# Attention scores in split precision: a low-by-low product left out, the low part taken in half-height products, and one division moved from DVE to GpSimd

## The chip, the cores and the metric

The kernel runs on one core of a Trainium2 chip. The metric is the device time of one execution in microseconds (us), lower is better. Engines are named as in the profile: PE is TensorE (its weight loads are listed apart as PEld), DVE is VectorE, ACT is ScalarE, POOL is GpSimd, SP issues most of the DMA transfers.

## The reference

Attention with a learned bias on the relative position, followed by two feed-forward layers, in float32:

```python
batch, n_heads, seq, head_dim = (2, 8, 576, 64)

scores = scale * np.matmul(q, k.transpose(0, 1, 3, 2))
x = (psi_rel / psi_i)[..., None]                     # positions only
bias = np.maximum(x @ w1 + b1, 0.0) @ w2
scores = scores + bias.transpose(2, 0, 1)[None]
scores = scores - np.max(scores, axis=-1, keepdims=True)
attn = np.exp(scores)
attn = attn / (np.sum(attn, axis=-1, keepdims=True) + 1e-09)
x = np.matmul(attn, v)                               # to (1152, 512)

g = x @ w_gate                                       # 512 -> 1536
x = (g / (1 + np.exp(-g)) * (x @ w_val)) @ w_out     # 1536 -> 512
h = x @ w_in                                         # 512 -> 2048
out = (np.maximum(h, 0) + np.log1p(np.exp(-np.abs(h)))) @ w_out2
```

## The kernel before

The program has three stages: the bias over positions (the first 55 us or so), attention, and the two feed-forward layers. The last two thirds are a long run of matmuls on PE (lines 722, 771 and 1080), whose order on PE is written out by hand; in attention the order on all engines is.

**Units and chunks.** A unit is one pair of heads of one batch element; there are eight. The queries of a unit go in two halves (`sub` 0 and 1), and a half is cut into chunks of 128 query rows against all 576 keys: four in the first half, five in the second, of which one (`"mix"`) takes the last 64 rows of both heads. So a unit has eight regular chunks and one mix chunk. A chunk's scores stand in a PSUM tile `ps` of two banks, one for each 288 keys (`hf` 0 and 1, `HALF` is 288).

**Precision.** A float32 matmul takes PE two instructions. The first two units (`i < PLAIN`) do that: `plain_scores` (line 313) multiplies the 64 head dimensions as they are. Inputs arrive with the 64 dimensions twice, in partitions 0 to 63 and again in 64 to 127, so one product runs in the upper half of the PE array (for `hf` 0) while one runs in the lower (for `hf` 1). From the third unit on, values are split into a high part and a remainder (the low part) in `float32r`, a form that PE multiplies in one instruction. `ql` and `qh` hold the low and high part of the queries, each twice over the 128 partitions. The key tile `kst` holds high parts in one half of the partitions and low parts in the other: for keys 0 to 287 the high parts lie in partitions 0 to 63, for keys 288 to 575 in partitions 64 to 127. A product of `ql` or `qh` over all 128 partitions thus adds the products with the keys' high and low parts in one go. `kst` and `ql` get their low parts from POOL (line 197).

**A slot.** `run_slot` issues one chunk: its scores on PE (`scores`, line 340), what DVE does with them (line 363: bias, scale and row maximum, PSUM to SBUF as `e`), the exponential of the chunk before on ACT (line 377), the sum and its reciprocal on DVE (381, 384), and the division of the row by its sum (line 388), which is on POOL but for one chunk. Then PE transposes pieces of a chunk that is three slots older (`pt`, line 414), ACT or DVE copy them to SBUF (`at`, line 421), and when all pieces of a half are there, PE multiplies them by the values (`po`, line 441). `finish` (lines 461 to 498) reads `po` out. The PSUM pool of `ps` has two tiles, that of `po` one. On PE, scores are thus always followed by transposes, except for the very last chunk, which is followed by `po`.

**Array shapes.** In the rows below, a matmul's first numbers are the partitions that it contracts over and the columns of the array that it uses. Scores of the plain units are 64x128 (two side by side), those of later units and transposes 128x128, `po` 128x64 (two side by side), the bias stage 128x32 (four side by side).

**The end of attention.** The last unit's half 1 has its fifth chunk (`n == 4`) divided on DVE. Behind that, in DVE's order, stand `t` and `B21l` (line 461), which read the `po` of half 0, a copy of transposed pieces (421), and the conversion of the first feed-forward weights (693, 696).

Of the kernel before, what the change touches and what calls it, by code (L numbers as in the profile page):

```python
# [15 lines left out]
ALU = mybir.AluOpType  # L16
# [3 lines left out]
P = 128  # L20
B, H, S, D, HID = 2, 8, 576, 64, 32
NP = H // 2
# [29 lines left out]
HALF = S // 2  # L52
# [47 lines left out]
def rows(w, f):  # L100

    return w.bitcast(I32)[P * f : P * (f + 1)].rearrange("p (k f) -> p k f", k=NK)
# [3 lines left out]
def tile_kernel(ctx: ExitStack, tc, qT, kT, vS, vT, wg, wv, wo, wi, wo2, table, out):  # L106
    nc = tc.nc
# [23 lines left out]
    with ExitStack() as actx:  # L131
# [166 lines left out]
        def plain_scores(u, n):  # L298


            sub, pr = u["sub"], u["pr"]
            ch = u["chunks"][n]
            ps = psS.tile([P, 2, 512], F32, tag="S", name="ps")
            if ch[0] == "mix":
                parts, bt = [(0, 0, 512), (1, 1, 256), (0, 1, 512), (1, 0, 256)], bias[4][:, pr]
            else:
                a, c = ch
                o, bt = 256 * sub + D * (sub and a) + P * c, bias[2 * sub + c][:, 2 * pr + a]
                parts = [(a, hf, o) for hf in range(2)]
            for a, hf, o in parts:  # L310
                rows = slice(D * hf, D * (hf + 1))
                to, m = (slice(D * a, D * (a + 1)), D) if ch[0] == "mix" else (slice(None), P)
                nc.tensor.matmul(  # L313
                    ps[to, hf, :HALF],
                    u["qr"][rows, a, o : o + m],
                    u["kr"][rows, a, HALF * hf : HALF * (hf + 1)],
                    start=True,
                    stop=True,
                )
            return ps, bt  # L320

        def scores(u, n):

            if u["i"] < PLAIN:
                return plain_scores(u, n)
            sub, pr, kst = u["sub"], u["pr"], u["kst"]
            ch = u["chunks"][n]
            ps = psS.tile([P, 2, 512], F32, tag="S", name="ps")
            if ch[0] == "mix":
                heads = [(0, 256), (1, 320)]  # L330
                bt = bias[4][:, pr]
            else:
                a, c = ch
                heads = [(a, (448 if sub else 256) * a + P * c)]
                bt = bias[2 * sub + c][:, 2 * pr + a]

            parts = [(t, a, o) for t in ("ql", "qh") for a, o in heads]
            for hf in range(2):
                for i, (t, a, o) in enumerate(parts):
                    nc.tensor.matmul(  # L340
                        ps[:, hf, :HALF],
                        u[t][:, o : o + P],
                        kst[:, a, HALF * hf : HALF * (hf + 1)],
                        start=i == 0,
                        stop=i == len(parts) - 1,
                    )
            return ps, bt

        marks = {}
# [25 lines left out]
        def softmax(u, n):  # L375
            e, sm = u["es"][n][:, :S], u["sm"]
            nc.scalar.activation(e, e, AF.Exp, bias=sm[:, 0, n : n + 1], scale=-1.0, accum_out=u["sums"][:, n, :1])  # L377
            for batch in BATCHES[u["sub"]]:
                if batch[-1] == n:
                    cols = slice(batch[0], n + 1)  # L380
                    nc.vector.tensor_reduce(
                        out=sm[:, 1, cols], in_=u["sums"][:, cols], axis=mybir.AxisListType.X, op=ALU.add
                    )
                    nc.vector.reciprocal(sm[:, 2, cols], sm[:, 1, cols])  # L384
                    for i in batch:
                        e = u["es"][i][:, :S]
                        eng = nc.vector if u["i"] == 2 * NP - 1 and n == 4 else nc.gpsimd
                        eng.tensor_scalar(e, e, sm[:, 2, i : i + 1], 1.0, op0=ALU.mult, op1=ALU.mult)  # L388

        made = [0, 0]  # L390

# [139 lines left out]
        def run_slot():  # L531
            nonlocal turned, done, prep, before, slot
            got = None
            if slot < len(chunks):
                i, sub, n = chunks[slot]
                if n == 0:
                    for _ in prep:
                        pass
                    if (i, sub) == (1, 0):
                        load_v(units[1])  # L540
                    elif (i, sub) == (0, 1):
                        units.append(load_k(2))
                    elif sub and i + 1 < 2 * NP:
                        load_q(units[i + 1])
                        if i > 1:
                            load_v(units[i + 1])
                        prep = itertools.chain(prepare_k(units[i + 1]), prepare_q(units[i + 1], 0))
                    elif i > 1 and not sub:
                        if i + 1 < 2 * NP:
                            units.append(load_k(i + 1))  # L550
                        if i == 2:
                            load_v(units[2])
                            units[2][0].update(v=units[2]["v"], vt=units[2]["vt"])
                        prep = prepare_q(units[i], 1)
                    if i < PLAIN:
                        job(units[i], sub)
                    if i == NP and sub == 0:
                        flat = lambda ap: ap.rearrange("p a s -> p (a s)")
                        pairs[2:] = [flat(bias[c][:, 2 * a : 2 * a + 2]) for a in range(2) for c in (2, 3)]
                        mixes[1] = flat(bias[4][:, :2])[:, : 5 * P]  # L560
                        nc.gpsimd.memset(mixes[1][:, S:], 0.0)
                u = units[i][sub]
                got = scores(u, n) if slot < len(chunks) - 1 else None
# [10 lines left out]
            if before:  # L574
                softmax(*before)
                before = None
# [14 lines left out]
            if slot == len(chunks) - 2:  # L591
                i, sub, m = chunks[-1]
                biased(units[i][sub], m, *scores(units[i][sub], m))
                softmax(u, n)
                softmax(units[i][sub], m)
# [497 lines left out]
    with tc.manual_schedule(engines={E.PE}):  # L1093
        quads = {"z": z}
        for q in range(4):
# [5 lines left out]
            for word in f"{OTHER if q else FIRST} {TAIL}".split():  # L1101
                who, what = word
                if who in "tu":
                    n = int(what)
                    if ws is None:
                        ws = convert(first + 2, outs[0]) + convert(first + 3, outs[1])
                    if q == 3 and n == 4:
                        t = TOKENS[n][0]
                        a = acc[t // 2][:, t % 2]
                        for at in (slice(0, DM // 2), slice(DM // 2, DM)):  # L1110
                            if who == "t":
                                held[n, at.start] = wide()[:, 0]
                            ps = held[n, at.start]
# [9 lines left out]
                    for i, t in enumerate(TOKENS[n]):  # L1123
                        if who == "t":
                            continue
                        a, ps = acc[t // 2][:, t % 2], held[n][:, i]
# [57 lines left out]
```

## Time and profile before

| | |
|---|---|
| three runs | 585.14, 585.31, 585.14 us; median 585.14 |
| the profiled execution | 585.39 us, of which 583.6 us from its first to its last instruction |
| attention with split products | 77.3 to 169.3 us of the span |
| end of attention | 169.3 to 184.5 us |
| feed-forward layers | 184.5 to 583.6 us |
| PE busy | 573.3 us (98% of the span), at the full granted clock |

Times in the rows count from the start of the span. PE's instructions overlap in the array, so a busy time is no sum of costs: what an instruction costs is the distance from its start to the start of the next one.

### The profile page before, as it was taken

What the parts mean: (1) busy time and instruction counts of PE and PEld (TensorE: products, weight loads), DVE (VectorE), ACT (ScalarE), POOL (GpSimd) and SP (SyncE); (2) the same over time, 40 slices, a digit from 0 to 9 for tenths busy, and PEclk for the clock granted to TensorE, in tenths of its full rate; (3) what the DMA queues carried; (4) which work ended last, traced back from release to release, by engine and by line L of the source; (5) the groups of instructions that cost most, each with busy time, mean ns of one, the idle gap of its engine ahead of it and who ended that gap; (6) DMA issues with size and microseconds to landing.
All of it is one profiled execution on the core that took longest, in us unless ns stands there. A gap on an engine that the chain in (4) does not pass through costs nothing.

```text
span 583.6 us, 11330 instructions
## 1 busy us (share of the span) xinstructions
PE 573.3 (98%) x4282; PEld 504.9 (87%) x4282; DVE 445.2 (76%) x958; ACT 377.1 (65%) x717; POOL 104.1 (18%) x160
## 2 busy tenths in 40 slices
PE   8999999999999999999999999999999999999997
PEld 5334588888888999999999999999989989988986
DVE  7999677778789989978879626589998876974432
ACT  7999888888887867656568325369727715733520
POOL 1002588898890000000000000000000000000000
PEclk9999999999999999999999999999999999999999
DMA  8999624233233342332343231222243241310013
GB/s 309 213 206 211 168 82 129 88 112 113 72 109 112 113 138 74 108 109 74 112 142 110 79 120 45 103 87 73 85 164 114 73 144 36 111 36 1 1 51 113
DMA packets 42039, 63.32 MB, mean 108 GB/s; under 512 B 4096, under 2 KB 30976, under 8 KB 41984
## 3 DMA queue, kind: packets, MB, share of 16 engines
q1 hardware_dynamic: 41984, 62.59, 36.9%
q8 instruction: 34, 0.56, 0.4%
q14 instruction: 21, 0.17, 0.1%
HBM read 49.60 MB, written 2.36 MB: 89 GB/s over the span
## 4 chain that ended last, share of the span: by engine, by line
PE 86%; ACT 6%; DVE 3%; DMA 2%; issue 1%; POOL 1%; DVEq 0%; ACTq 0%; POOLq 0%
PE pw L771 38%; PE pw L1080 17%; PE pw L722 13%; PE po L441 6%; PE ps L340 5%; PE pt L414 4%; ACT early L289 2%; ACT r L267 2%; PE pb L277 2%; PE ps L313 1%; DMA bias<-early 1%; DVE e L363 1%; DVE r L269 1%; ACT e L377 1%; POOL e L388 1%
## 5 line engine op out<-in xcount | busy, mean ns | idle before, releaser
L1080 PE MATMUL pw<-oh,g2h 128*128 128x512 f32 (+1 forms) x148 | 56.9, 384 | 0.0
L1080 PE MATMUL pw<-oh,g2l 128*128 128x512 f32 (+1 forms) x148 | 56.9, 384 | 0.0
L1080 PE MATMUL pw<-ol,g2h 128*128 128x512 f32 (+1 forms) x148 | 56.8, 384 | 0.0
L722 PE MATMUL pw<-gl,sh 128*128 128x384 f32 x144 | 48.2, 335 | 0.0
L722 PE MATMUL pw<-gh,sl 128*128 128x384 f32 x144 | 48.2, 334 | 0.0
L722 PE MATMUL pw<-gh,sh 128*128 128x384 f32 x144 | 48.2, 334 | 0.0
L696 DVE SCALAR_TENSOR_TENSOR x<-raw,x 128x512 int32<-128x512 int32 x68 | 46.2, 687 | 0.8
L277 PE MATMUL pb<-r,G 128*32 128x288 f32 x576 | 43.2, 416 | 3.4 <-ACT early L289 0.8
L363 DVE CUSTOM_DVE_ANT_0 e<-ps,bias 128x576 f32<-128x576 f32 x44 | 33.0, 751 | 16.3 <-PE ps L340 11.3
L388 POOL TENSOR_SCALAR e<-e,sm 128x576 f32<-128x576 f32 x43 | 33.1, 778 | 60.1 <-DVE sm L384 45.4
L269 DVE TENSOR_SCALAR r<-G 128x576 f32<-128x576 f32 x96 | 42.0, 522 | 0.0
L277 PEld LDWEIGHTS pb<-r,G 128*32 128x32 f32 x576 | 16.8, 110 | 28.9 <-ACT early L289 16.5
L421 ACT COPY at<-pt 128x512 f32<-128x512 f32 (+2 forms) x69 | 36.4, 550 | 7.5 <-PE pt L414 7.3
L441 PE MATMUL po<-at,v 128*64 128x256 f32 (+3 forms) x384 | 36.8, 332 | 1.3 <-issue 1.3
L340 PE MATMUL ps<-kst,ql 128*128 128x288 f32 x120 | 36.8, 335 | 0.5 <-POOL ql L197 0.4
L377 ACT ACTIVATE e<-e,sm 128x576 f32<-128x576 f32 x44 | 34.3, 780 | 2.9 <-DVE sm L363 1.4
L1130 DVE TENSOR_TENSOR acc<-pw,acc 128x512 f32<-128x512 f32 x26 | 16.8, 685 | 23.6 <-PE pw L1080 23.6
L693 DVE TENSOR_SCALAR x<-x 128x512 int32<-128x512 int32 x68 | 28.4, 423 | 8.4 <-ACT x L691 5.0
L441 PEld LDWEIGHTS po<-at,v 128*64 128x64 f32 x384 | 26.9, 137 | 8.2 <-issue 3.5
L1080 PEld LDWEIGHTS pw<-oh,g2l 128*128 128x128 f32 x148 | 27.8, 188 | 5.6
L1080 PEld LDWEIGHTS pw<-ol,g2h 128*128 128x128 f32 x148 | 27.8, 188 | 5.1
L1080 PEld LDWEIGHTS pw<-oh,g2h 128*128 128x128 f32 x148 | 27.8, 188 | 5.0
(274 smaller groups left out, 1677.3 us busy)
## 6 DMA issues: line engine op xcount, KB each, us to landing
raw<-in_wo_dram SPq DMA_DIRECT2D x28, 512.0 KB, 3.5
bias<-early SPq DMA_DIRECT2D x32, 288.0 KB, 8.4
raw<-in_wi_dram SPq DMA_DIRECT2D x16, 512.0 KB, 4.0
raw<-in_wv_dram SPq DMA_DIRECT2D x12, 512.0 KB, 4.2
raw<-in_wg_dram SPq DMA_DIRECT2D x12, 512.0 KB, 3.5
qr<-in_qT_dram SPq DMA_DIRECT2D x7, 576.0 KB, 3.8
bias<-in_kT_dram SPq DMA_DIRECT2D x6, 576.0 KB, 4.5
v<-in_vS_dram SPq DMA_DIRECT2D x8, 384.0 KB, 3.2
```

The costliest lines, as they stand in the source:

```text
L269: nc.vector.tensor_scalar(r, src[:, w0 : w0 + S], PB[:, n : n + 1], 0.0, op0=ALU.add, op1=ALU.max)
L277: nc.tensor.matmul(pb[32 * ct : 32 * ct + 32, hf, :HALF], W2, rs[ct][:, HALF * hf : HALF * (hf + 1)], start=True, stop=True,)
L340: nc.tensor.matmul(ps[:, hf, :HALF], u[t][:, o : o + P], kst[:, a, HALF * hf : HALF * (hf + 1)], start=i == 0, stop=i == len(parts) - 1,)
L363: nc.vector.tensor_tensor_reduce(out=e[:, :S].rearrange("p (a n) -> p a n", a=2), in0=ps[:, :, :HALF], in1=bt.rearrange("p (a n) -> p a n" ...
L377: nc.scalar.activation(e, e, AF.Exp, bias=sm[:, 0, n : n + 1], scale=-1.0, accum_out=u["sums"][:, n, :1])
L388: eng.tensor_scalar(e, e, sm[:, 2, i : i + 1], 1.0, op0=ALU.mult, op1=ALU.mult)
L421: marks[eng, u["i"], u["sub"]] = copy(at[:, :w], pt[:, :w]).ins
L441: nc.tensor.matmul(u["po"][D * a : D * (a + 1), o : o + n], v[:, D * t : D * (t + 1)], at[:, i : i + n], start=piece == 0 and o == 0, stop ...
L696: nc.vector.scalar_tensor_tensor(yi, lw, 29, yi, op0=ALU.logical_shift_right, op1=ALU.bitwise_or)
L722: nc.tensor.matmul(ps[:, :n], w[:, k], x, start=first and k == 0 and i == 0, stop=last and k == NK - 1 and i == 2)
L771: nc.tensor.matmul(ps[:, hf, :HALF], a[:, o + k], b[:, HALF * hf : HALF * (hf + 1)], start=start and k == 0 and i == 0, stop=k == 1 and i ...
L1080: nc.tensor.matmul(ps[:, at], g, w.rearrange("p k f -> p (k f)")[:, at], start=f == 0 and i == 0, stop=f == 3 and i == 2)
```

## The change

In `scores`, `qh` now comes ahead of `ql`, the loop over `hf` is the inner one, and `ql` is multiplied only in the 64 partitions in which `kst` holds high parts: the product of the low parts of queries and keys is left out. For `hf` 0 this is a product in the upper half of the array, for `hf` 1 in the lower, each into its own PSUM bank. The number of matmuls is the same. In `softmax`, the one division that was on DVE goes to POOL like the others.

```diff
@@ scores
-            parts = [(t, a, o) for t in ("ql", "qh") for a, o in heads]
-            for hf in range(2):
-                for i, (t, a, o) in enumerate(parts):
-                    nc.tensor.matmul(
-                        ps[:, hf, :HALF],
-                        u[t][:, o : o + P],
-                        kst[:, a, HALF * hf : HALF * (hf + 1)],
-                        start=i == 0,
-                        stop=i == len(parts) - 1,
-                    )
+            for t, rows in ("qh", lambda hf: slice(None)), ("ql", lambda hf: slice(D * hf, D * (hf + 1))):
+                for i, (a, o) in enumerate(heads):
+                    for hf in range(2):
+                        nc.tensor.matmul(
+                            ps[:, hf, :HALF],
+                            u[t][rows(hf), o : o + P],
+                            kst[rows(hf), a, HALF * hf : HALF * (hf + 1)],
+                            start=t == "qh" and i == 0,
+                            stop=t == "ql" and i == len(heads) - 1,
+                        )
@@ softmax
-                        eng = nc.vector if u["i"] == 2 * NP - 1 and n == 4 else nc.gpsimd
-                        eng.tensor_scalar(e, e, sm[:, 2, i : i + 1], 1.0, op0=ALU.mult, op1=ALU.mult)
+                        nc.gpsimd.tensor_scalar(e, e, sm[:, 2, i : i + 1], 1.0, op0=ALU.mult, op1=ALU.mult)
```

Lines behind the second edit move up by one: 414 becomes 413, 441 becomes 440, 461 becomes 460.

PE in the third unit, a regular chunk, transposes, the mix chunk (its two heads together) and the transposes behind it. Before:

```order
L340 MATMUL ps<-kst,ql 128x288
L340 MATMUL ps<-kst,qh 128x288
L340 MATMUL ps<-kst,ql 128x288
L340 MATMUL ps<-kst,qh 128x288
L414 MATMUL pt<-ident,e_898 128x128 x4
L340 MATMUL ps<-kst,ql 128x288 x2
L340 MATMUL ps<-kst,qh 128x288 x2
L340 MATMUL ps<-kst,ql 128x288 x2
L340 MATMUL ps<-kst,qh 128x288 x2
L414 MATMUL pt<-ident,e_897 128x128
```

The same place after the change:

```order
L340 MATMUL ps<-kst,qh 128x288 x2
L340 MATMUL ps<-kst,ql 128x288 x2
L413 MATMUL pt<-ident,e_898 128x128 x4
L340 MATMUL ps<-kst,qh 128x288 x4
L340 MATMUL ps<-kst,ql 128x288 x4
L413 MATMUL pt<-ident,e_897 128x128
```

The rows name the shape of the result, so that they don't show the height: the `qh` products stay 128x128, the `ql` products are now 64x128, and what follows, a transpose, is 128x128 again.

DVE at the end of attention, from the last reciprocals on. Before:

```order
L381 TENSOR_REDUCE sm_103<-sums_107 128x1
L384 RECIPROCAL sm_103<-sm_103 128x1
L388 TENSOR_SCALAR e_116<-e_116,sm_103 128x576
L461 TENSOR_TENSOR t<-po,t2f 128x320
L461 TENSOR_TENSOR B21l<-po,B21h 128x320
L421 COPY at<-pt 128x512
```

POOL's last instructions after the change:

```order
L581 TENSOR_TENSOR T2l<-t2f,T2h 128x320
L387 TENSOR_SCALAR e_115<-e_115,sm_103 128x576 x2
L581 TENSOR_TENSOR T3l<-t3f,T3h 128x320
L387 TENSOR_SCALAR bias_84<-bias_84,sm_103 128x576
L387 TENSOR_SCALAR e_116<-e_116,sm_103 128x576 x2
```

DVE loses its row of line 388, and everything behind it moves up; POOL's last row was a single one and is now two in a row.

## Rows read from the trace of the kernel before

**Rows 1.** The page: busy time by engine.

```profile
PE 573.3 (98%) x4282; PEld 504.9 (87%) x4282; DVE 445.2 (76%) x958; ACT 377.1 (65%) x717; POOL 104.1 (18%) x160
```

**Rows 2.** Busy time by stage: split-product attention, feed-forward.

```profile
core 0: us, PE busy (x) PEld busy (x) DVE busy (x) ACT busy (x) POOL busy (x), PEclk, DMA share, GB/s
77.30:169.30 92.00, 91.57 (x819) 80.84 (x819) 69.70 (x232) 80.42 (x195) 81.78 (x120) 1.00 0.35 109
...
184.50:583.60 399.10, 396.07 (x2559) 378.60 (x2558) 295.67 (x527) 214.60 (x372) 0.00 (x0) 1.00 0.28 90
```

**Rows 3.** Timeline of PE, a regular chunk between transposes (start, length, instruction).

```profile
140.12 0.40 PE L340 MATMUL ps<-kst,ql 128*128 128x288 f32 x1
140.36 0.29 PE L340 MATMUL ps<-kst,qh 128*128 128x288 f32 x1
...
141.76 0.29 PE L340 MATMUL ps<-kst,qh 128*128 128x288 f32 x1
141.89 0.29 PE L340 MATMUL ps<-kst,ql 128*128 128x288 f32 x1
142.02 0.30 PE L340 MATMUL ps<-kst,qh 128*128 128x288 f32 x1
142.16 0.60 PE L414 MATMUL pt<-ident,bias 128*128 128x128 f32 x4
```

**Rows 4.** Timeline of PE, then PEld: a plain chunk of 64x128 products between transposes.

```profile
59.38 0.27 PE L414 MATMUL pt<-ident,e 128*128 128x128 f32 x1
59.59 0.51 PE L313 MATMUL ps<-kr,qr 64*128 64x288 f32 x2
...
59.93 0.41 PE L313 MATMUL ps<-kr,qr 64*128 64x288 f32 x2
...
60.27 0.33 PE L414 MATMUL pt<-ident,e 128*128 128x128 f32 x1
...
60.44 0.38 PE L414 MATMUL pt<-ident,e 128*128 128x128 f32 x2
...
59.58 0.30 PEld L313 LDWEIGHTS ps<-kr,qr 64*128 64x128 f32 x4 [0.17 <-issue]
60.27 0.31 PEld L414 LDWEIGHTS pt<-ident,e 128*128 128x128 f32 x3 [0.39 <-issue]
```

**Rows 5.** Timeline of PE, bias stage, rounds of four 128x32 products: four rounds between the rows.

```profile
50.20 0.67 PE L277 MATMUL pb<-r,G 128*32 128x288 f32 x8
...
51.17 0.67 PE L277 MATMUL pb<-r,G 128*32 128x288 f32 x8
```

**Rows 6.** Timeline of PE at the last chunk, followed by 128x64 products.

```profile
169.11 0.29 PE L340 MATMUL ps<-kst,qh 128*128 128x288 f32 x1
169.33 0.48 PE L441 MATMUL po<-at,v 128*64 128x320 f32 x2
```

**Rows 7.** Waits of PEld, 77.3 to 169.3 us (total, times, longest), and one by itself.

```profile
PEld ps L340 <- DVE sm L363: 2.1, 7, 0.4
...
PEld ps L340 <- POOL ql L197: 0.9, 2, 0.5
...
114.96 0.19 PEld L340 LDWEIGHTS ps<-kst,ql 128*128 128x128 f32 x1 [0.39 <-DVE sm L363]
```

**Rows 8.** Timeline of each engine at the end of attention.

```profile
172.04 2.68 DVE L388 TENSOR_SCALAR e<-e,sm 128x576 f32<-128x576 f32 x1
174.65 0.47 DVE L461 TENSOR_TENSOR t<-po,t2f 128x320 f32<-128x320 f32 x1
175.04 0.47 DVE L461 TENSOR_TENSOR B21l<-po,B21h 128x320 fp32r<-128x320 f32 x1
...
173.67 0.74 POOL L388 TENSOR_SCALAR e<-e,sm 128x576 f32<-128x576 f32 x1
...
175.62 0.83 PE L441 MATMUL po<-at,v 128*64 128x256 f32 x5 [1.31 <-issue]
...
181.04 0.66 PE L414 MATMUL ps<-ident,e 128*128 128x128 f32 x4
```

## The prediction

> **What bounds the kernel now.** I read the page first: PE is busy 98% of the span, no other engine over 76% [rows 1]. An average over stages proves little, so the stages came next. In the 92.0 us of split-product attention PE is busy 91.57 at the full granted clock (1.00, so 2.4 GHz); ACT has 80.42, POOL 81.78, DVE 69.70 [rows 2]. POOL and ACT are not far behind, but PE has no slack: what lengthens its list of instructions there lengthens the stage. In the feed-forward layers PE is busy 396.07 of 399.10 and the other engines have room [rows 2]; that stage keeps its length and starts earlier or later.
>
> A busy time hides what happens between two matmuls, so I went on to the timeline of PE and read distances from start to start. In a regular chunk the split products start 0.13 us apart (141.76, 141.89, 142.02), and the first transpose stands 0.14 behind the last of them [rows 3]. Transposes are 0.11 apart: four of them take 0.60, the last 0.27 of it, which leaves 0.33 for three steps [rows 3]. There is no hole between 128x128 instructions, whatever they compute.
>
> Where the shape of the array changes, there is one. The plain chunks of the first two units are the only place with 64x128 products, the shape that `ql` gets. Their four instructions are two passes of a side-by-side pair [rows 4]. What a pass streams is seen in the bias stage, where rounds of the same 288 columns follow each other without a change of shape: 0.97 us for four, 0.24 each [rows 5]. Against that:
>
> - last transpose to first pair 0.21 (59.38 to 59.59), where a transpose streams 0.11: 0.10 idle;
> - first pair to second 0.34 (59.59 to 59.93) where 0.24 are streamed: 0.10, the first pair's weights, which nothing covers;
> - second pair to transpose 0.34 (59.93 to 60.27): 0.10 idle again;
> - first transpose to second 0.17 (60.27 to 60.44) instead of 0.11: 0.06 of uncovered load.
>
> PEld shows the same from its side: its loads come behind idle times of 0.17 and 0.39 that end on "issue", so on no other engine [rows 4]. The shape costs two changes, in and out.
>
> **The change, scores.** Each regular chunk had four products on the full array. It keeps two (`qh`), and the two `ql` products run side by side in one stream. That removes 0.13 per regular chunk, 0.26 per mix chunk (eight products become four and two pairs). The price is two changes of shape, because the `qh` products ahead and the transposes behind are 128x128.
>
> Does that price hold for split products? Two rows say so. The last chunk is followed by 128x64 products, and they start 0.22 behind its last product (169.11 to 169.33), 0.09 over its stream [rows 6]. And the first split product behind a change of shape is 0.24 ahead of the second (140.12 to 140.36), so 0.11 of its load is uncovered [rows 3]. I take 0.09 + 0.10 + 0.10 + 0.06 = 0.35 per chunk, with the idle time in from the split row and the rest from the plain chunk, the only one with both directions.
>
> Six units have 48 regular and 6 mix chunks, and all but the very last are followed by transposes. Regular: 0.35 - 0.13 = +0.22, times 47, 10.3. Mix: 0.35 - 0.26 = +0.09, times 6, 0.5 (the second pair's weights load while the first streams). The last regular chunk changes shape behind its scores already; it gains one idle time and one load, 0.09 + 0.10 - 0.13 = +0.06. Together +10.9 us of PE.
>
> The idle time at a change is the largest part. The Trainium skill ("TensorE: Matmul & The Clock Gate", part 2, step 4) lets the last column take some 128 cycles through the array, an estimated 0.05 us at 2.4 GHz; with 0.05 for each of the two idle times, the scores would cost about 4.5 us less. The rows have 0.09 to 0.10, and no row has less.
>
> **What is given back.** PE does wait now and then. Its loads for scores waited 2.1 us on `sm` (line 363, DVE has to release a `ps` tile), 7 times, and 0.9 on `ql` from POOL, twice [rows 7]. Three of the seven, such as that at 114.96, are 0.39 long and stand right behind `po` products, where a change of shape costs as much with no wait; that leaves 2.1 - 1.2 = 0.9 for DVE. A chunk that occupies PE 0.22 us longer leaves DVE that much more time per tile, and the waits are 0.2 to 0.3 each; `ql` is now needed two products and one idle time later (0.26 + 0.09). So nearly all goes: I take 1.8 of these 1.8 us. The bounds are 0 and 2.3, with the short waits that the list leaves out. Nothing new waits: DVE and ACT take each chunk later but have more time for it, and the chunk behind the scores is three slots old.
>
> **The change, division.** The DVE division takes 2.68 us (172.04 to 174.72), and it ends when POOL's last division does (173.67 + 0.74 = 174.41, then 0.31) [rows 8]. It starts as POOL works through three instructions; it looks held until POOL is through, which one row can't prove. Behind it are `t` and `B21l`, which read `po`; `B21l` ends at 175.51, and the next `po` product, for which there is no second tile, starts at 175.62 after 1.31 us of idle PE [rows 8]. With the division on POOL, DVE comes to `t` some 2.6 us earlier and PE has its tile when its transposes end. I take -1.3, PE's idle time. POOL divides this chunk at about 174.4 to 175.2, and its transposes come at 181.04 [rows 8]: 5 us of cover. Should the conversions that now reach DVE earlier be held by POOL in the same way, 0.7 us of the 1.3 is gone; the bounds are 0 and -1.5.
>
> **Sum.** 10.9 - 1.8 - 1.3 = +7.8. The profiled execution took 585.39 us, 1.79 of it outside its span of 583.6; it stands 0.25 over the median. So 585.39 + 7.8 = 593.2 by it, and 592.9 against the median.
>
> **Rivals.** A measurement of this kernel can tell about 0.2%, 1.2 us, from no change.
>
> *A change between split products is free* (the faster side). Then the scores save 47 x 0.13 + 6 x 0.26 + 0.13 = 7.8, and with the division it is 585.1 - 7.8 - 1.3 = 576.0; PE would wait more for DVE, which may take back 2. For it: no row has a split product on both sides of a change. Against it: rows 6 and the 0.24 of rows 3 have one on one side and pay in full. It decides at the price per chunk at which 54 chunks cost what is saved and given back, (7.8 + 1.8 + 1.3) / 54 = 0.20 us; below that the kernel is faster. The Trainium skill ("TensorEngine Tiling (Array Packing)", overview) promises up to twice the rate for contractions of 64 and less; the same page says that a change of mode drains the engine, without a price.
>
> *Weights are loaded ahead over a change.* Then only the idle times are paid, 0.19: 54 x 0.16 = 8.6 less, so 10.9 - 8.6 - 1.8 - 1.3 = -0.8, 584.3. Rows 4 show loads that begin with their matmul, not ahead. The Trainium skill ("TensorE: Matmul & The Clock Gate", part 2, step 1) has PE pull weight loads ahead of running matmuls where row groups don't conflict or the second weight buffer is the target; by it this case would hold, by the rows it doesn't.
>
> *Half-height split products run one after the other.* Each pair costs 0.13 more: 48 x 0.13 + 6 x 0.26 = 7.8, 600.7. Rows 4 show two instructions per pass in the time of one, in plain float32; I see no reason for a difference.
>
> *PE is not the bound.* If ACT or POOL set the pace, the scores cost nothing, and 583.8 is left. The 91.57 of 92.0 speak against it.
>
> **How the numbers follow.** The forecast gets 0.80, free changes 0.08, the other three 0.04 each. The forecast's own bounds: nothing given back and nothing from the division is +10.9, 596.0, with a second uncovered load per mix chunk 596.6; all 2.3 and 1.5 back and no uncovered load at the first transpose (54 x 0.06 = 3.2) is +3.9, 589.0. As the forecast has 0.8 by itself, this is the range, 589 to 597. Slower by over 0.2%: forecast and serial pairs, 0.84. Faster: free changes and half of the unbound case, 0.10. The rest, 0.06, is no difference.
>
> **What would show it.** Line 340 has 120 `ql` rows of 64x128 in pairs that start within 0.01 us. From the last `qh` to the first `ql` there are about 0.22 us, from the `ql` pair to the first transpose about 0.33, and 0.17 to the second. The stretch from the first split product to the start of the feed-forward layers, 77.4 to 184.5 now, is 7 to 8 us longer, and that behind it keeps its 399.1. At the end of attention, no DVE instruction takes 2.7 us, and PE's 1.31 us of idle time is gone. The prediction is wrong if `ql` follows `qh` after 0.13 us, or if the pairs don't start together.

## The result and the profile after

The changed kernel takes 592.11 us (median of 4 runs, 591.93 to 593.33) against 585.18 for the kernel before on the same chip: ratio 1.0121, 95% interval 1.0109 to 1.0134. It is slower by 6.9 us; 592.9 was forecast, in a range of 589 to 597. The profiled execution took 592.11 us too, with a span of 590.3.

The stages by busy time (start and end, length, then busy time and number of instructions of PE, PEld, DVE, ACT and POOL, the granted clock, DMA), cut where the first split product, the first of the last values and the feed-forward layers start:

```profile
76.80:177.40 100.60, 100.60 (x824) 74.80 (x822) 70.01 (x233) 81.17 (x199) 83.31 (x122) 1.00 0.31 100
177.40:191.20 13.80, 13.80 (x140) 10.62 (x138) 10.86 (x28) 11.11 (x25) 4.31 (x6) 1.00 0.26 78
191.20:590.30 399.10, 396.08 (x2559) 378.74 (x2558) 295.58 (x527) 214.27 (x372) 0.00 (x0) 1.00 0.28 90
```

Against [rows 2] the stage of split products grew from 92.0 to 100.6 us, and it starts 0.5 earlier. The end of attention shrank from 15.2 (169.3 to 184.5) to 13.8. The feed-forward layers have the same 399.1. So 8.6 - 0.5 - 1.4 = +6.7, the difference of the two spans. PE's busy time in the first row is its whole length, which is no sign of work: matmuls overlap, and what lies between them can be seen only from their starts.

The timeline of PE in the changed kernel, from the last transpose ahead of a regular chunk to the mix chunk (start, length, instruction; names as in [rows 3]):

```profile
84.66 0.27 PE L413 MATMUL pt<-ident,e 128*128 128x128 f32 x1
84.69 0.51 PE L340 MATMUL ps<-kst,qh 128*128 128x288 f32 x2
...
84.91 0.29 PE L340 MATMUL ps<-kst,qh 128*128 128x288 f32 x1
85.13 0.40 PE L340 MATMUL ps<-kst,ql 64*128 64x288 f32 x2
85.46 0.44 PE L413 MATMUL pt<-ident,e 128*128 128x128 f32 x2
...
87.49 0.77 PE L340 MATMUL ps<-kst,qh 128*128 128x288 f32 x4
88.19 0.53 PE L340 MATMUL ps<-kst,ql 64*128 64x288 f32 x4
88.65 0.44 PE L413 MATMUL pt<-ident,e 128*128 128x128 f32 x2
```

And PEld at the same regular chunk:

```profile
85.13 0.18 PEld L340 LDWEIGHTS ps<-kst,ql 64*128 64x128 f32 x2 [0.16 <-issue]
85.46 0.20 PEld L413 LDWEIGHTS pt<-ident,e 128*128 128x128 f32 x2
85.63 0.14 PEld L413 LDWEIGHTS pt<-ident,m 128*128 128x128 f32 x1
```

The row at 84.91 is the second of the two `qh` products that the row at 84.69 counts. From it to the `ql` products there are 0.22 us, and these are one row of two because they start together (all 60 pairs within 0.01 us). From them to the first transpose there are 0.33 us (85.13 to 85.46), of which one stream is 0.13: the rest is a load that nothing covers and an idle time. The next transpose follows after 0.17 (85.46 to 85.63) instead of 0.11. In the mix chunk the second pair adds 0.13 (0.46 from 88.19 to 88.65), so its load is covered. From the last transpose before the scores to the first behind them a regular chunk takes 0.80 us (84.66 to 85.46); the same stretch takes 0.64 with full-height products (experiment 3 shows it at the same place). With the slower second transpose that is 0.16 + 0.06 = 0.22 us more.

### The profile page after: what moved, and what is told of

Same layout as the page of the kernel before. It is cut to its first block, busy times and chain, and to the rows that moved or that the text cites. A ratio compares the mean times of both kernels' runs of the same rounds, so it can differ in the third digit from the quotient of the medians.

```text
span 590.3 us, 11314 instructions
## 1 busy us (share of the span) xinstructions
PE 581.3 (98%) x4282; PEld 498.9 (85%) x4282; DVE 442.2 (75%) x957; ACT 376.4 (64%) x717; POOL 104.4 (18%) x161
## 4 chain that ended last, share of the span: by engine, by line
PE 92%; ACT 4%; DMA 1%; DVE 1%; issue 1%; POOL 0%; DVEq 0%; POOLq 0%
PE pw L770 38%; PE pw L1079 17%; PE pw L721 13%; PE pt L413 7%; PE po L440 7%; PE ps L340 6%; ACT early L289 2%; ACT r L267 2%; PE ps L313 2%; PE pb L277 2%; DMA bias<-early 1%; DVE r L269 1%; DMA G<-in_table_dram 1%; PE ps L413 0%; ACT r L263 0%
## 5 line engine op out<-in xcount | busy, mean ns | idle before, releaser
L413 PE MATMUL pt<-ident,e 128*128 128x128 f32 x188 | 33.6, 287 | 0.1
```

The source lines that it names most:

```text
L413: nc.tensor.transpose(pt[:, P * w : P * (w + 1)], e, ident)
```

## The experiments

**1 and 2: each edit alone.** First the division alone:

```diff
-                        eng = nc.vector if u["i"] == 2 * NP - 1 and n == 4 else nc.gpsimd
-                        eng.tensor_scalar(e, e, sm[:, 2, i : i + 1], 1.0, op0=ALU.mult, op1=ALU.mult)
+                        nc.gpsimd.tensor_scalar(e, e, sm[:, 2, i : i + 1], 1.0, op0=ALU.mult, op1=ALU.mult)
```

> The kernel before with its one DVE division on POOL, scores untouched. Theory (DVE held PE up by 1.3 us at the end of attention): PE's 1.31 us of idle time ahead of the last unit's first values is gone, 585.2 - 1.3 = 583.8 us. Rival (another wait takes its place, or the division costs nothing either way): 585.2.

Measured: 584.21 us (11 runs, 583.78 to 584.55) against 585.21, ratio 0.998 (0.9971 to 0.9989). The end of attention in its profile:

```profile
169.10:182.90 13.80, 13.80 (x139) 10.63 (x138) 11.26 (x30) 11.52 (x27) 5.76 (x8) 1.00 0.27 79
```

It is 1.4 us shorter than before, and PE has no idle time in it. The profiled execution (583.78) shows the whole gain, the median 1.0 us of it: the theory holds in its mechanism, and its 583.8 is what the fastest of the runs take.

Then the scores alone, as in the diff of the change, with the division left on DVE.

> The changed scores with the division still on DVE. Theory (the two edits add up): 592.1 + 1.3 = 593.4 us. Rival (the later scores shift the end of attention so that the division no longer holds PE): 592.1.

Measured: 592.32 us against 585.21, ratio 1.0121 (1.0107 to 1.0134). The rival is right: with the changed scores, the place of the division is worth 0.2 us, which is no difference. DVE, POOL and ACT's copy of `po` at the end of attention in this kernel:

```profile
179.63 0.16 DVE L384 RECIPROCAL sm<-sm 128x1 f32<-128x1 f32 x1
179.83 0.87 DVE L388 TENSOR_SCALAR e<-e,sm 128x576 f32<-128x576 f32 x1
181.19 0.49 DVE L461 TENSOR_TENSOR t<-po,t2f 128x320 f32<-128x320 f32 x1 [0.48 <-ACT B21h L466]
...
177.36 1.47 POOL L388 TENSOR_SCALAR e<-e,sm 128x576 f32<-128x576 f32 x2
178.79 0.88 POOL L582 TENSOR_TENSOR T3l<-t3f,T3h 128x320 fp32r<-128x320 f32 x1
179.64 0.75 POOL L388 TENSOR_SCALAR bias<-bias,sm 128x576 f32<-128x576 f32 x1
180.36 0.96 POOL L388 TENSOR_SCALAR e<-e,sm 128x576 f32<-128x576 f32 x1
...
180.66 0.42 ACT L466 CAST B21h<-po 128x320 fp32r<-128x320 f32 x1 [0.68 <-PE po L441]
```

POOL at the same place in the kernel before, whose DVE division ran from 172.04 to 174.72:

```profile
170.67 1.46 POOL L388 TENSOR_SCALAR e<-e,sm 128x576 f32<-128x576 f32 x2
172.10 0.86 POOL L582 TENSOR_TENSOR T3l<-t3f,T3h 128x320 fp32r<-128x320 f32 x1
172.95 0.74 POOL L388 TENSOR_SCALAR bias<-bias,sm 128x576 f32<-128x576 f32 x1
```

The same instruction that took 2.68 us [rows 8] takes 0.87. It starts while POOL is in `bias`, ends 0.31 behind it (180.70 against 180.39), and POOL's next division takes 0.96 instead of 0.74. So it passed between two POOL instructions. In the kernel before it began at 172.04, just before POOL's second `e` ended (172.13), and came through only behind the three that followed, with which POOL was done. DVE is free 0.48 us before `t` can start (the idle time in its row), and the end of attention is 13.8 us here too. Passing early is not all of it: POOL is further ahead here. Its two `e` divisions start 0.16 us ahead of PE's first `po` product (177.52), where in the kernel before they started 1.34 behind it (169.33). Had POOL's last division held DVE again, `t` would have started at about 181.4 instead of 181.19, an estimate from these rows (180.36 + 0.74 + 0.31), and `B21l` would still have ended ahead of PE's next `po` product at 182.43.

**3: the order without the shape.** `ql` comes second, as in the changed kernel, but in full height:

```diff
-            for t, rows in ("qh", lambda hf: slice(None)), ("ql", lambda hf: slice(D * hf, D * (hf + 1))):
+            for t, rows in ("qh", lambda hf: slice(None)), ("ql", lambda hf: slice(None)):
```

> The changed kernel, the order of the four products kept (both qh, then both ql), but ql over all 128 partitions, so that no product leaves the 128x128 shape and the low-by-low product is computed again. Theory (the shape costs the time, the order none): no gap between products, 0.13 us from each to the next, 0.5 to 0.9 us of waits on ql gone as ql comes two products later, and the division's 1.3: 583.0 to 583.4 us. Rival (the order, with two products of one weight tile next to each other, is what costs): 590 or more.

Measured: 583.59 us (7 runs, 583.46 to 584.05) against 585.21, ratio 0.9973 (0.9962 to 0.9984). It beats the kernel before and the changed one; it has neither the changes of shape ahead of and behind `ql` nor the held division. The timeline of PE at the chunk shown above:

```profile
83.91 0.27 PE L413 MATMUL pt<-ident,e 128*128 128x128 f32 x1
83.94 0.51 PE L340 MATMUL ps<-kst,qh 128*128 128x288 f32 x2
84.28 0.43 PE L340 MATMUL ps<-kst,ql 128*128 128x288 f32 x2
84.55 0.27 PE L413 MATMUL pt<-ident,e 128*128 128x128 f32 x1
```

No hole, 0.64 us from transpose to transpose. The waits of PEld in this stage (total, times, longest):

```profile
PEld ps L340 <- DVE sm L363: 2.3, 7, 0.4
...
PEld ps L340 <- POOL ql L197: 0.2, 1, 0.2
```

Of the 0.9 us on `ql` [rows 7] 0.2 is left; those on DVE are all there. The order, then, is a small gain; the 0.6 us between the medians of experiments 1 and 3 is no more than their runs scatter, so its size stays open. Half height in place of full height costs 592.11 - 583.59 = 8.5 us, with the saved streams and the waits given back already in it.

**4: twice as many changes of shape.** The same products, each half-height one right behind the full one of its own half of the keys:

```diff
-            for t, rows in ("qh", lambda hf: slice(None)), ("ql", lambda hf: slice(D * hf, D * (hf + 1))):
-                for i, (a, o) in enumerate(heads):
-                    for hf in range(2):
+            for i, (a, o) in enumerate(heads):
+                for hf in range(2):
+                    for t, rows in ("qh", slice(None)), ("ql", slice(D * hf, D * (hf + 1))):
```

> The changed kernel, each half-height ql product right behind the qh product of its own half of the keys: the same products, but in a regular chunk four changes of shape where there were two, in a mix chunk eight, and no two half-height products side by side. Theory (0.19 us into the half height, 0.21 back to a split product, 0.16 back to a transpose): a regular chunk 0.53 longer than with the change, a mix chunk 1.46, 592.1 + 48 x 0.53 + 6 x 1.46 = 626 us. Rival (the cost hangs on the half-height products themselves, not on the change of shape): only side by side is lost, 592.1 + 7.8 = 600.

Measured: 634.11 us (median of 4; 631.8 twice, 636.4 and 636.6) against 585.21, ratio 1.0835 (1.080 to 1.087). The rival's 600 is out. The timeline of PE in a regular chunk:

```profile
89.05 0.38 PE L340 MATMUL ps<-kst,qh 128*128 128x288 f32 x1
89.36 0.39 PE L340 MATMUL ps<-kst,ql 64*128 64x288 f32 x1
89.68 0.40 PE L340 MATMUL ps<-kst,qh 128*128 128x288 f32 x1
90.01 0.40 PE L340 MATMUL ps<-kst,ql 64*128 64x288 f32 x1
```

Every product is 0.31 to 0.33 us from the one before it, where without a change it is 0.13: a change between two split products, in either direction, costs about 0.20 us at that place. That is the price expected, but the time is 5.8 us over the expected 626 in two runs and some 10.5 in the other two. The windows point to the clock (columns as above; the clock stands behind POOL):

```profile
91.90:94.90 3.00, 3.00 (x12) 1.76 (x11) 1.23 (x6) 0.98 (x4) 1.96 (x4) 1.00 0.00 0
94.90:97.90 3.00, 3.00 (x21) 2.66 (x21) 1.37 (x3) 1.94 (x5) 2.76 (x4) 0.50 0.02 5
98.40:101.40 3.00, 3.00 (x28) 2.08 (x25) 0.00 (x0) 0.42 (x1) 0.00 (x0) 1.00 0.22 55
...
77.00:217.00 140.00, 139.97 (x821) 95.31 (x819) 69.75 (x233) 85.29 (x200) 84.62 (x124) 0.95 0.23 72
```

In the second window the granted clock is 0.50, that is 1.2 GHz; the stage has four such stretches. Over the 140.0 us of the stage it is 0.95 in the mean, so the engine lost 0.05 of 140, 7.0 us of full clock, which is room enough for the 5.8 of the profiled execution (631.79). What made the other two runs longer has no profile. The kernel before and the changed one have 1.00 in this stage.

**5: no `ql` products at all.** The scores are `qh` times `kst` alone, without the low parts of the queries:

```diff
-            for t, rows in ("qh", lambda hf: slice(None)), ("ql", lambda hf: slice(D * hf, D * (hf + 1))):
-                for i, (a, o) in enumerate(heads):
-                    for hf in range(2):
-                        nc.tensor.matmul(
...
+            for i, (a, o) in enumerate(heads):
+                for hf in range(2):
+                    nc.tensor.matmul(
+                        ps[:, hf, :HALF],
+                        u["qh"][:, o : o + P],
+                        kst[:, a, HALF * hf : HALF * (hf + 1)],
+                        start=i == 0,
+                        stop=i == len(heads) - 1,
+                    )
```

> The changed kernel with the ql products left out altogether: scores from the third unit on are qh times the keys' high and low parts alone (the low parts of the queries are still made, but not used). No product leaves the 128x128 shape, and PE loses two of four streams: 48 x 0.26 + 6 x 0.52 = 15.6 us. Theory (PE sets the pace of this stage, the others are close behind): ACT's 80.4 and POOL's 81.8 us of work in the stage of 92.0 take over, and 6 to 10 us come back: 574 to 578 us. Rival (PE alone counts, no other engine near): 583.6 - 15.6 = 568. Rival (PE is not the bound): 583 to 584, as without the change of shape.

Measured: 580.02 us against 585.58, ratio 0.9905 (0.9892 to 0.9919). All three numbers miss. Against experiment 3, PE has 15.6 us less to stream, and the kernel gains 3.6, or 3.9 if each is taken against the kernel before beside it (5.56 against 1.62). The stage in this profile and what PE and PEld waited for in it:

```profile
77.00:165.00 88.00, 79.66 (x704) 65.15 (x704) 70.27 (x233) 80.07 (x199) 81.83 (x120) 1.00 0.37 115
```

```profile
PEld ps L339 <- DVE sm L362: 8.4, 14, 1.4
PEld pt L412 <- POOL e L386: 3.2, 4, 1.5
...
PE ps L339 <- DVE sm L362: 3.9, 6, 1.1
PE pt L412 <- POOL e L386: 2.1, 3, 1.3
...
DVE e L362 <- PE ps L339: 7.2, 6, 1.8
DVE bias L362 <- PE ps L339: 5.9, 5, 1.8
```

No engine is busy for the 88.0 us, ACT and POOL neither, so the theory's reason fails with its number. PE now waits for DVE to release `ps` tiles and for POOL's divisions ahead of the transposes, while DVE waits for PE's scores: engines wait for each other by turns. PE is the bound of this stage in the kernel before, but only by some 4 us. Which wait would have to go first is not shown.

**6: three divisions on DVE.** The last three divisions of attention on DVE, so that POOL has little behind the point where DVE starts:

```diff
-                        eng = nc.vector if u["i"] == 2 * NP - 1 and n == 4 else nc.gpsimd
+                        eng = nc.vector if u["i"] == 2 * NP - 1 and u["sub"] and n >= 3 else nc.gpsimd
```

> The kernel before with the last three divisions of attention on DVE instead of the last one alone; POOL keeps one subtraction (T3l) there and nothing behind it. Theory (the 2.68 us were waiting for POOL's three instructions, not work): the first division ends about 0.3 us behind T3l, the next two take 0.3 to 0.5 each, B21l ends 0.5 to 0.9 earlier than before, 584.3 to 584.8 us. Rival (DVE is slow at this division by itself): three of 2.7 us, B21l some 5 us later, 589 to 590.

Measured: 585.23 us (11 runs) against 585.58, ratio 0.9995 (0.9986 to 1.0005), no difference. DVE's divisions and what POOL does meanwhile:

```profile
171.18 2.02 DVE L388 TENSOR_SCALAR bias<-bias,sm 128x576 f32<-128x576 f32 x1
173.12 0.51 DVE L388 TENSOR_SCALAR e<-e,sm 128x576 f32<-128x576 f32 x1
...
173.92 0.52 DVE L388 TENSOR_SCALAR e<-e,sm 128x576 f32<-128x576 f32 x1
174.36 0.48 DVE L461 TENSOR_TENSOR t<-po,t2f 128x320 f32<-128x320 f32 x1
174.76 0.48 DVE L461 TENSOR_TENSOR B21l<-po,B21h 128x320 fp32r<-128x320 f32 x1
...
170.53 1.50 POOL L388 TENSOR_SCALAR e<-e,sm 128x576 f32<-128x576 f32 x2
171.97 0.91 POOL L582 TENSOR_TENSOR T3l<-t3f,T3h 128x320 fp32r<-128x320 f32 x1
```

The first division ends at 173.20, 0.32 behind POOL's last instruction (171.97 + 0.91 = 172.88); the two with POOL idle take 0.51 and 0.52. So the division is half a microsecond of DVE, and by the two ends just behind a POOL instruction (0.31 in the kernel before, 0.32 here) the rest of 2.68 was waiting. The rival is out. `B21l` ends only 0.27 us earlier than before (175.24 against 175.51), less than the 0.5 to 0.9 expected, and it has three divisions ahead of it now. PE still stands idle for 1.15 us ahead of the same values instead of 1.31, so the expected 584.3 to 584.8 is missed; the 0.35 us between the two medians is not clear of their scatter.

## Why the prediction was right

**The price of a change of shape** was right in each part: 0.22 us from the last `qh` to the `ql` pair, 0.33 from there to the first transpose, 0.17 to the second, and pairs that start together. That the rows of plain float32 hold for split products was the assumption with most weight. It held, and experiments 3 and 4 show it from both sides, with 0.64 us instead of 0.80 for the same chunk without changes, and about 0.20 more for each further one. The 0.05 us that the prediction estimated for the idle time from the Trainium skill ("TensorE: Matmul & The Clock Gate", part 2, step 4) is below what this trace has: 0.22 less a stream of 0.13 is 0.09. Nor does any row show a weight load pulled ahead over a change, which step 1 of that part of the Trainium skill would allow: the loads at 85.13 and 85.46 start with their matmuls.

**The sum for the scores** holds too. The rows of two decimals leave 0.01 us per chunk open, so the starts were added up over all chunks of both traces, in nanoseconds: a regular chunk costs PE 0.213 us more up to the second transpose, a mix chunk 0.084, the last chunk 0.064, together 10.6 us where 10.9 was forecast. **What is given back** was the mis-sized term: 1.8 was taken. The stage grew by 8.6, of which 0.5 is an earlier start, so by 8.1 us, and 10.6 - 8.1 leaves 2.5 given back; the upper bound had been 2.3. The starts show where it comes from. In the kernel before, eight chunks start 0.15 to 0.55 us behind the transpose ahead of them, where the others start 0.03 behind; the eight together take 2.4 us longer for it. In the changed kernel every chunk behind a transpose starts 0.03 behind it. So all the waits went, the short ones too that the list leaves out. The list of waits of PEld in the changed kernel, 76.8 to 177.4 us, shows what is left ahead of scores:

```profile
PEld ps L340 <- issue: 12.8, 64, 0.4
...
PEld ps L340 <- POOL ql L197: 0.2, 1, 0.2
```

DVE is gone from it [rows 7]. The rest is "issue": 53 loads of the first `ql` pair of a chunk and 11 loads behind `po` products, all at changes of shape. Three of those behind `po` stood under DVE in the kernel before, as the prediction had read them.

**The division** was forecast at -1.3, and the end of attention is 1.4 us shorter. The reason given was only half right. It was right that DVE stood waiting for POOL (experiment 6) and that PE's 1.31 us hung on it (experiment 1). It was wrong that DVE comes to `t` 2.6 us earlier. In experiment 1, without the division, `t` has a wait of its own:

```profile
172.75 0.49 DVE L460 TENSOR_TENSOR t<-po,t2f 128x320 f32<-128x320 f32 x1 [0.99 <-POOL T3l L581]
172.23 0.42 ACT L465 CAST B21h<-po 128x320 fp32r<-128x320 f32 x1 [0.27 <-PE po L440]
```

Its row names POOL's `T3l`, from which `t` reads nothing. It starts 0.10 us behind the end of ACT's copy of the same `po`, and in experiment 2, where the row names that copy, 0.11 behind it; so the copy is the likelier cause. Counted from the start of the stage, `t` comes 1.7 us earlier, which was still enough for PE. And the two edits don't add up: experiment 2 has the division on DVE and the same 13.8 us; with the later scores POOL is further ahead. The scores alone cost 592.32 - 585.21 = 7.1 us, where 10.9 - 1.8 = 9.1 was forecast, and the division next to them is worth 0.2 us, nothing that can be measured, where 1.3 was forecast. These two misses, 2.0 and 1.1 us, have opposite signs and partly cancel in the sum, 6.9 against 7.8. So the price of the shape is why the sum was right; that the split between the two edits did not spoil it is luck.

**The rivals.** Free changes, loads ahead of a change and serial pairs are each ruled out by the timeline above (0.33 from pair to transpose, loads that start with their matmul, pairs in one row). That PE is not the bound is ruled out where its work grows, as here; where it shrinks, experiment 5 shows that the others are close behind. This corrects the first rival, which set up to 2 us of new waits against 7.8 us of savings: with twice the savings only 3.6 came through, so free changes would by that have won less than the forecast 9 us; no run has them.

## What to carry to other kernels

A pair of half-height products saves a stream but pays for two changes of shape, here 0.35 us against 0.13. Two pairs in a row (the mix chunk) still lose 0.08; by these numbers (no run tried it) three would about break even. The price stands in any stretch of the trace where shapes alternate already, read from start to start, since busy times count the holes. And before taking work off the engine that is the bound, ask how close the next chain is: here about 4 us.

## What the runs showed of the hardware

- PE's granted clock fell to 1.2 GHz four times in experiment 4 although PE had work all the time. Ahead of the fall, PE did little but half-height and full products by turns, each behind an idle time; ahead of the rise it ran the `po` products, which follow each other without one. What exactly makes it fall stays open. The changed kernel, with half as many changes, kept 1.00.
- A DVE division of 128x576 values took 0.51 us with POOL idle, 0.87, 2.02 and 2.68 with POOL at work in SBUF. With POOL at work it ended 0.3 us behind a POOL instruction each time, but not behind the same one: in experiment 2 it came in behind the one that was running, in the kernel before and in experiment 6 only behind POOL's last. What decides that stays open.
- The division on POOL alone (experiment 1) gave 583.8 to 583.9 in five runs and 584.2 to 584.6 in six; no run shows what differs.
